# Low halves of second-layer weights: from TensorE to VectorE

## The chip, the cores and the metric

The kernel runs on one core of one Trainium2 chip. The core has five engines that run side by side, each through its own list of instructions in a fixed order, and wait for one another by semaphores: TensorE (PE in the profile), VectorE (DVE), ScalarE (ACT), GpSimd (POOL) and SyncE (SP), which issues all the transfers here. The metric is the device time of one execution in microseconds (us).

## What is computed

A recurrence over 768 positions for 4 x 8 pairs of batch and head (a delta rule with a 48 x 48 state), then two layer pairs on the 3072 tokens:

```python
for t in range(S):
    kt, vt, bt = (k_n[:, :, t], v[:, :, t], beta[:, :, t, None])
    y[:, :, t] = np.einsum('bhd,bhde->bhe', q[:, :, t], state)
    v_old = np.einsum('bhde,bhd->bhe', state, kt)
    state = state + bt[:, :, :, None] * np.einsum('bhd,bhe->bhde', kt, vt - v_old)
...
h = x @ w_in                       # 384 -> 1024
solu = h * softmax(h)
ln = (solu - mu) / np.sqrt(var + 1e-06) * g_ln
x = ln @ w_out                     # 1024 -> 384
...
h = x @ w_in                       # 384 -> 2048, second layer
g = h * (1.0 / (1.0 + np.exp(-1.702 * h)))
out = g @ w_out                    # 2048 -> 384
```

## The kernel before

The sequence is cut into 24 chunks of 32 positions, so that the recurrence becomes 24 steps. Four chunks make a group of 512 tokens. The Plan class gives each piece of work a tag, by which the text names it: `gram` (products of keys with keys and queries, L568, masked by VectorE in L583), `solve` (inverse of a triangular matrix for four chunks on VectorE, with 60 elimination operations in L642 and L645), `rec` (one recurrence step), `A` (first layer and normalisation of one chunk), `B` (first layer's output product of a group, L946) and `C` (second layer of a group, products L981 up and L1008 down).

One recurrence step is a chain over several engines. TensorE forms the state's product with the keys (L748), VectorE subtracts it (L752), in the first four steps TensorE solves twice (L765, then L770 after a copy by ScalarE, and L776 on VectorE), TensorE solves (L757), ScalarE and VectorE copy the result (L782, L786), TensorE forms the output (L792) and the state's update (L827 in the early steps, L822 later), and VectorE adds that to the state (L836), from where the next step goes on. A chunk's layer A then runs through L874 on TensorE, L881 and L893 on VectorE, L890 on ScalarE, and its last lines on GpSimd (L911, L923) and ScalarE. B of a group needs all four chunks; its result is rounded to a high half on ScalarE (L950) and a low half on VectorE (L953), and C needs both. In C, VectorE (L989) and GpSimd (L995) form the halves of the activation.

Products are made of fp16 halves: each operand is high + low, and three of the four products are summed. So each weight tile (128 x 512 of w1 and w2, 128 x 384 of wo1 and wo2; 6 + 8 of the first layer, 12 + 16 of the second) must be turned into two fp16 tiles. The weights arrive as 64-bit floats. Each tile is loaded (L476), rebuilt as fp32 by one ScalarE operation (L479) and three VectorE operations (L481, L483, L491), rounded to the high half by ScalarE (L504), and the low half, the residual, is formed in one of two ways. `PRM["pe"]` is the number of tiles, in the order of their making, that take the first way:

```python
        if nst[0] <= PRM["pe"]:
            bk = Bank((6, 7, 5, 4, 3))

            def rest():
                PE.matmul(bank(bk)[:, 0:n], lhsT=eye[:, (WS, W2S).index(sc)], rhs=fv, start=True, stop=False)
                PE.matmul(bank(bk)[:, 0:n], lhsT=neg, rhs=dh, start=False, stop=True)
            P.add("PE", 1.1 * n / 512, rest, r=fk + [wk + "h", "eye"], w=[bk], prio=prio)
            P.add("ACT", act(n), lambda: ACT.activation(out=dl, in_=bank(bk)[:, 0:n], func=ACTF.Copy),
                  r=[bk], w=[wk + "l"] + over("l"), prio=prio)
        else:
            P.add("DVE", dve(n), lambda: DVE.scalar_tensor_tensor(
                out=dl, in0=fv, scalar=sc, in1=dh, op0=ALU.mult, op1=ALU.subtract),
                r=fk + [wk + "h"], w=[wk + "l"] + over("l"), prio=prio, port=True)
```

The first way is two matmuls, with a scaled unit matrix (L510) and a negative one (L511), and a copy out of PSUM by ScalarE (L513); the second is one VectorE operation (L516).

The order of the work on every engine is set by a planner when the program is built. Each piece has a priority; to it is added an entry of the table `OFF`, by tag and engine. The planner walks through time with its own durations and at each moment starts the ready piece with the lowest priority. Where it expects TensorE to wait before the first C has begun, it puts filler matmuls on zeros into TensorE's list (L351), whose result nobody reads. On the chip each engine only follows its list.

Of the kernel before, what the change touches and what calls it, by code (L numbers as in the profile page):

```python
# [34 lines left out]
PRM = dict(bl=161.965, vm=-0.684, vo=-1.262, pe=38.322, near=22.976, al=0.0, af=0.658, xp=25.764, lp=1.945, go1=24.87, so1=49.904, ew=48, nx=6.743, kp=13.711, need=100.793, fg=0.161, f1=7.669, f3=1796.849, sp=0.084, gp=0.667, gq=99, cold=25.151, cf=-1.14, nb4=9.499, v1b=1.424, cut=0.473, el=22.0, la=0.602, d0=-55.31, d1=-18.518, d2=6.18, d3=1.2, a0=14.438, wo1s=1.606, nk=15.164, nb2=1.269, nb3=7.307, early=21.447, v1=-9.577, wa=0.829, U=36.161, T0=31.882, g0=0.697, a=-0.318, b=0.937, ao=18.661, go=231.282, gs=-2.989, so=-0.04, ss=0.661, w1=-840.745, wo1=-7.28, w2o=-52.255, w2s=8.446, wo2o=41.493, wo2s=4.056, nb=1.319, bs=0.333, cs=4.152, su=8.832, ld=47.69)  # L35
# [24 lines left out]
class Clock:  # L60
# [12 lines left out]
    def behind(self, at):  # L73

        return PRM["need"] * (1.0 - (self.end - at) / self.TICK) - self.sum

# [14 lines left out]
class Plan:  # L91
# [14 lines left out]
    def add(self, eng, dur, fn, r=(), w=(), prio=0.0, lat=0.0, small=False, nb=0.0, work=1.0, port=None):  # L106
        t = Task()
        t.eng, t.dur, t.fn, t.prio, t.lat = eng, dur, fn, prio + OFF.get(self.tag, 0.0) + OFF.get(f"{self.tag}|{eng}", 0.0), lat
        t.deps, t.outs, t.end, t.left, t.ready = set(), [], None, 0, nb
# [26 lines left out]
    def emit(self, sem=SEM, log=None):  # L136
# [6 lines left out]
        top = max(t.work2 for t in self.tasks)  # L143
        if PRM["al"]:
            for t in self.tasks:
                t.prio = (1 - PRM["al"]) * t.prio + PRM["al"] * PRM["af"] * (top - t.work2)
        free = {}
# [19 lines left out]
        while done < n:  # L167
            cand = None
            for e, ts in pend.items():
# [4 lines left out]
                for t in ts:  # L174
                    st = max(e0, t.ready)
                    if t.lat:
                        st = max(st, dma_free - PRM["la"])
                    ok = True
# [22 lines left out]
            if t.eng == "PE":  # L201
                small, near = t.small, t.prio + PRM["near"]
            pend[t.eng].remove(t)
# [5 lines left out]
            if t.eng == "PE":  # L209
                for gate, until, filler in self.fill:  # L210
# [3 lines left out]
                    while True:  # L214
                        clock.run(lo, 0.0, 1.0)
                        if not (st - lo > (PRM["fg"] if clock.warm else 0.5) or clock.warm and clock.behind(lo) > 0.0):
                            break
# [873 lines left out]
```

## Time and profile before

| | us |
|---|---|
| three runs, median | 839.51 |
| lowest and highest of them | 835.08 and 845.69 |
| the profiled execution | 836.79 |
| its span, first to last instruction | 835.1 |
| outside the span | 1.7 |

The profiled execution is one run of its own. Its views give, for each engine, when an instruction ran and what it had waited for. A line number (L516) is that of the kernel's file. Matmuls overlap in TensorE, so that the step from one start to the next tells what one costs there, and not its own duration. In the rows PE is TensorE, DVE VectorE, ACT ScalarE, POOL GpSimd.

### The profile page before, as it was taken

The numbers are of one execution on the slowest core, as the hardware profiler recorded it, in microseconds if no ns is written. First come the engines' busy times: TensorE is split into PE (matmuls) and PEld (weight loads), VectorE is DVE, ScalarE is ACT, GpSimd is POOL, SyncE is SP. The second block draws the span as 40 slices with busy tenths as digits, with TensorE's granted clock in tenths as the row PEclk, the third lists the DMA queues.
The fourth block names the chain that finished last, engine by engine and source line by source line (L and its number), as shares of the span: only waits on it lengthen the run. The fifth ranks groups of instructions, "written<-read, shape, count | busy, mean of one in ns | idle before, by whom it ended". The sixth has DMA issues, their size and how long they took to land.

```text
span 835.1 us, 25208 instructions
## 1 busy us (share of the span) xinstructions
PE 777.1 (93%) x10642; PEld 389.7 (47%) x10642; DVE 589.5 (71%) x1456; ACT 373.1 (45%) x661; POOL 247.2 (30%) x240
## 2 busy tenths in 40 slices
PE   6568978999989999998999999999999999999997
PEld 4135554444555444544544444444444444444443
DVE  2896777999999999999999899964566445212111
ACT  0467564544326524544633545525554355422332
POOL 3020011110413354325531434504442222420322
PEclk7778898999999999999999999999999999999999
DMA  6898597976646466677736654365433252100101
GB/s 168 235 278 232 148 220 137 235 196 168 125 94 139 86 149 171 147 177 159 168 79 187 142 119 104 84 152 144 103 79 94 80 115 44 26 1 0 39 1 38
DMA packets 177314, 105.76 MB, mean 127 GB/s; under 512 B 128273, under 2 KB 161169, under 8 KB 177201
## 3 DMA queue, kind: packets, MB, share of 16 engines
q1 hardware_dynamic: 177200, 104.15, 52.7%
q8 instruction: 83, 1.36, 0.7%
q14 instruction: 31, 0.25, 0.1%
HBM read 66.16 MB, written 20.64 MB: 104 GB/s over the span
## 4 chain that ended last, share of the span: by engine, by line
PE 53%; DVE 27%; issue 9%; DMA 4%; ACT 3%; POOL 2%; POOLq 0%; SPq 0%; ACTq 0%; DVEq 0%
PE psum L1008 13%; PE psum L981 13%; PE psum L946 9%; PE psum L874 6%; DVE mv L836 4%; DVE trip L645 4%; DVE trt L642 4%; PE psum L568 3%; DVE th L989 2%; PE psum L351 2%; DVE mv L786 2%; DVE col L881 2%; PE psum L510 2%; ACT mv L782 2%; DVE eb L893 2%
## 5 line engine op out<-in xcount | busy, mean ns | idle before, releaser
L995 POOL TENSOR_TENSOR gl<-th,gh 128x512 f16<-128x512 f32 x90 | 107.3, 1192 | 236.0 <-ACT gh L992 167.8
L989 DVE SCALAR_TENSOR_TENSOR th<-th,psum 128x512 f32<-128x512 f32 x96 | 65.5, 683 | 89.0 <-ACT th L986 88.4
L1008 PE MATMUL psum<-gl,wo2h 128*128 128x512 f16 x288 | 109.1, 379 | 1.0 <-POOL gl L995 1.0
L1008 PE MATMUL psum<-gh,wo2h 128*128 128x512 f16 x288 | 109.5, 380 | 0.2 <-ACT gh L992 0.2
L981 PE MATMUL psum<-x2th,w2h 128*128 128x512 f16 x288 | 109.5, 380 | 0.1
L981 PE MATMUL psum<-x2th,w2l 128*128 128x512 f16 x288 | 109.1, 379 | 0.0
L981 PE MATMUL psum<-x2tl,w2h 128*128 128x512 f16 x288 | 109.1, 379 | 0.0
L1008 PE MATMUL psum<-gh,wo2l 128*128 128x512 f16 x288 | 109.1, 379 | 0.0
L986 ACT ACTIVATE th<-psum 128x512 f32<-128x512 f32 x96 | 56.9, 593 | 98.4 <-PE psum L981 93.6
L874 PE MATMUL psum<-w1h,xt 128*128 128x512 f16 x288 | 94.2, 382 | 1.5 <-DVE mv L836 0.8
L992 ACT ACTIVATE gh<-th 128x512 f16<-128x512 f32 x96 | 60.2, 627 | 68.9 <-DVE th L989 64.6
L1008 PEld LDWEIGHTS <-wo2h 128*128 128x128 f16 x576 | 56.2, 98 | 67.9 <-issue 2.1
L981 PEld LDWEIGHTS <-w2h 128*128 128x128 f16 x576 | 53.5, 98 | 62.0 <-issue 0.3
L642 DVE TENSOR_TENSOR trt<-trip 128x30 f32<-128x30 f32 (+9 forms) x150 | 71.3, 476 | 2.7
L645 DVE TENSOR_TENSOR trip<-trip,trt 128x30 f32<-128x30 f32 (+9 forms) x150 | 69.6, 464 | 2.4
L923 POOL TENSOR_TENSOR lnr<-eb,lnr 128x1024 f16<-128x1024 f32 x24 | 52.2, 2173 | 52.0 <-ACT lnr L921 52.0
L874 PEld LDWEIGHTS <-xt 128*128 128x128 f16 x432 | 40.0, 98 | 49.9 <-issue 2.5
L890 ACT ACTIVATE eb<-psum,col 128x512 f32<-128x512 f32 x48 | 36.9, 773 | 52.4 <-DVE col L886 52.1
L946 PE MATMUL psum<-lnth,wo1h 128*128 128x512 f16 x144 | 54.6, 379 | 0.4 <-DVE th L989 0.4
L874 PE MATMUL psum<-w1l,xt 128*128 128x512 f16 x144 | 54.8, 381 | 0.0
L946 PE MATMUL psum<-lnth,wo1l 128*128 128x512 f16 x144 | 54.6, 379 | 0.0
L946 PE MATMUL psum<-lntl,wo1h 128*128 128x512 f16 x144 | 54.6, 379 | 0.0
(210 smaller groups left out, 1246.6 us busy)
## 6 DMA issues: line engine op xcount, KB each, us to landing
kq<-kq SPq DMA_DIRECT2D x44, 192.0 KB, 4.4
stg<-w_in SPq DMA_DIRECT2D x11, 512.0 KB, 5.6
vt<-vt SPq DMA_DIRECT2D x24, 192.0 KB, 2.7
st<-qt SPq DMA_DIRECT2D x48, 96.0 KB, 2.9
kt<-kdr SPq DMA_DIRECT2D x48, 96.0 KB, 2.3
stg<-udr SPq DMA_DIRECT2D x48, 96.0 KB, 2.3
out<-ob SPq DMA_DIRECT2D x18, 256.0 KB, 2.7
ktr<-kd SPq DMA_DIRECT2D x46, 96.0 KB, 2.9
```

Of the source, the lines that this page charges most:

```text
L642: DVE.tensor_tensor(out=tv, in0=tri[:, lo:hi, j:j + 1].to_broadcast([128, nr, j]), in1=tri[:, j:j + 1, 0:j].to_broadcast([128, nr, j]), op ...
L645: DVE.tensor_tensor(out=tri[:, lo:hi, 0:j], in0=tri[:, lo:hi, 0:j], in1=tv, op=ALU.add)
L874: PE.matmul(bank(bh[j]), lhsT=x[:, k], rhs=w_[:, k, 512 * j:512 * j + 512], start=(k == 0 and i == 0), stop=(k == K0 - 1 and i == 2))
L890: P.add("ACT", act(512) + 0.34, lambda j=j, ev=ev: ACT.activation(out=ev, in_=bank(bh[j]), func=ACTF.Exp, bias=cl(3), scale=cl(0), accum_o ...
L923: P.add("POOL", pool(F1), lambda: POOL.tensor_tensor(out=lnr[1], in0=e_, in1=lnr[0], op=ALU.subtract), r=["lnrh"] + [f"eb{ie}_{j}" for j i ...
L946: PE.matmul(bank(ba)[:, 0:w_], lhsT=wo1[a][:, k, oc], rhs=lnt[b][:, k, tk], start=(k == 0 and i == 0), stop=(k == K1 - 1 and i == 2))
L981: PE.matmul(bank(bh)[:, 0:w_], lhsT=w2[a][:, k, fc], rhs=x2t[b][:, k, tk], start=(k == 0 and j == 0), stop=(k == K0 - 1 and j == 2))
L986: P.add("ACT", act(w_), lambda: ACT.activation(out=th, in_=bank(bh)[:, 0:w_], func=ACTF.Tanh, scale=0.851 / (X2S * W2S)), r=[bh], w=[f"th{ ...
L989: P.add("DVE", dve(w_), lambda: DVE.scalar_tensor_tensor(out=th, in0=th, scalar=1.0, in1=bank(bh)[:, 0:w_], op0=ALU.add, op1=ALU.mult), r= ...
L992: P.add("ACT", act(w_), lambda: ACT.activation(out=gh, in_=th, func=ACTF.Copy), r=[f"th{i}"], w=[f"gh{i}"], prio=base)
L995: P.add("POOL", pool(w_), lambda: POOL.tensor_tensor(out=gl, in0=th, in1=gh, op=ALU.subtract), r=[f"th{i}", f"gh{i}"], w=[f"gl{i}"], prio= ...
L1008: PE.matmul(bank(acc[o])[:, 0:w_], lhsT=wo2[a][:, f, oc], rhs=gb[i][b][:, 0:w_], start=(f == 0 and j == 0), stop=(f == K2 - 1 and j == 2))
```

## The change

Two tables differ, both one line each in the file; of the first only the start of the old and the new one is shown, of the second all entries but `pe` are equal.

```diff
-OFF = {'gram0|SP': 42.93, 'gram0|PE': 207.21, 'gram0|DVE': 422.4, 'gram1|SP': 9.79,
...
+OFF = {'gram0|SP': -56.29, 'gram0|PE': -67.28, 'gram0|DVE': 69.66, 'gram1|SP': 146.16,
...
-PRM = dict(bl=161.965, vm=-0.684, vo=-1.262, pe=38.322, near=22.976,
...
+PRM = dict(bl=161.965, vm=-0.684, vo=-1.262, pe=14, near=22.976,
...
```

With `pe` at 38.322 the first 38 tiles took the first way: all 14 of the first layer and 24 of the 28 of the second. With 14 only those of the first layer do, and L516 forms the residual of all 28 of the second. The entries of `OFF` are other numbers for nearly every tag and engine, so the order of all the work is another one. In the lists, L351 stands 232 times instead of 128, L510 and L511 belong to 14 tiles instead of 38, L513 stands 14 times instead of 38, L516 28 times instead of 4; all other lines are as many as before. Of the 232 fillers 222 stand ahead of B0, of the 128 126. 

TensorE, from the last state product of the third recurrence step to the fourth step's L770 (L827: state update; L568: a gram; `fst`: a rebuilt weight tile; `eye` and `neg`: the unit matrices). Before:

```order
L827 MATMUL psum_69<-mv,kt_118 48x48 x16
L510 MATMUL psum_68<-fst_88,eye 128x384
L511 LDWEIGHTS neg
L511 MATMUL psum_68<-wo2h,neg 128x384
L568 MATMUL psum_67<-kq_112 32x64 x32
L748 MATMUL psum_70<-mv,ktr_114 32x48 x32
L568 MATMUL psum_69<-kq_111 32x64 x32
L765 MATMUL psum_68<-rb_132,dt_130 32x48 x32
```

The changed kernel, same place, to L770:

```order
L827 MATMUL psum_68<-mv,kt_118 48x48 x16
L568 MATMUL psum_69<-kq_112 32x64 x32
L351 LDWEIGHTS zeros_157
L351 MATMUL psum_63<-zeros_157 128x512
L748 MATMUL psum_68<-mv,ktr_114 32x48 x32
L568 MATMUL psum_69<-kq_111 32x64 x32
L765 MATMUL psum_68<-rb_132,dt_130 32x48 x32
L351 LDWEIGHTS zeros_157
L351 MATMUL psum_63<-zeros_157 128x512
L770 MATMUL psum_69<-vt_121,dt_131 32x48 x32
```

The residual of a tile between L827 and L748 is gone, and a filler on `zeros` stands there and between L765 and L770; the 9 fillers between the first and the fourth step's L765 have become 48, and the 17 residuals in that stretch 2.

VectorE, among the elimination operations of the second solve, around the first L953 (`trip`, `trt`: the triangular matrix; `stg`, `fst`, `ob`: a weight tile as it arrives and as it is rebuilt; `w2l`, `wo2l`: low halves). Before, with the first L516 of all as the last row:

```order
L481 TENSOR_SCALAR stg_84<-stg_84 128x384
L642 TENSOR_TENSOR trt<-trip 128x238
L483 SCALAR_TENSOR_TENSOR fst_89<-fst_89,stg_84 128x384
L645 TENSOR_TENSOR trip<-trip,trt 128x14x17
L491 SCALAR_TENSOR_TENSOR fst_89<-stg_84,fst_89 128x384
L642 TENSOR_TENSOR trt<-trip 128x234
L953 SCALAR_TENSOR_TENSOR x2tl<-psum_66,x2th 128x512
L645 TENSOR_TENSOR trip<-trip,trt 128x13x18
L516 SCALAR_TENSOR_TENSOR wo2l<-fst_89,wo2h 128x384
```

The changed kernel, where the first L953 follows 8 rows further on:

```order
L491 SCALAR_TENSOR_TENSOR fst_87<-wo2l,fst_87 128x384
L642 TENSOR_TENSOR trt<-trip 128x238
L516 SCALAR_TENSOR_TENSOR w2l<-ob_109,w2h 128x512
L645 TENSOR_TENSOR trip<-trip,trt 128x14x17
L516 SCALAR_TENSOR_TENSOR wo2l<-fst_87,wo2h 128x384
L642 TENSOR_TENSOR trt<-trip 128x234
L481 TENSOR_SCALAR stg_84<-stg_84 128x384
```

Here L516 stands among rebuilding and elimination: between the fourth step's L752 and the third L953 there are 13 L516 instead of 1, 60 elimination operations instead of 51 and 38 rebuilding operations instead of 36; ahead of that L752, 9 L516 instead of none and 74 rebuilding operations instead of 87.

## Rows read from the trace of the kernel before

**Rows 1.** The page, part 1: busy us, share of span, instructions.

```profile
PE 777.1 (93%) x10642; PEld 389.7 (47%) x10642; DVE 589.5 (71%) x1456; ACT 373.1 (45%) x661; POOL 247.2 (30%) x240
```

**Rows 2.** Busy time by stretches; columns as the head row says.

```profile
core 0: us, PE busy (x) PEld busy (x) DVE busy (x) ACT busy (x) POOL busy (x), PEclk, DMA share, GB/s
61.60:125.50 63.90, 55.74 (x1504) 35.50 (x1504) 45.23 (x113) 39.98 (x80) 5.75 (x5) 0.88 0.83 203
125.50:175.90 50.40, 45.43 (x837) 24.54 (x834) 42.35 (x122) 23.52 (x40) 8.49 (x6) 0.94 0.94 181
175.90:200.80 24.90, 24.90 (x255) 11.98 (x257) 24.49 (x67) 10.93 (x20) 0.00 (x0) 1.00 0.63 174
200.80:540.00 339.20, 326.55 (x4847) 164.49 (x4836) 317.12 (x778) 155.27 (x271) 133.90 (x120) 1.00 0.60 137
540.00:835.10 295.10, 287.70 (x2629) 135.28 (x2627) 118.95 (x267) 119.06 (x205) 88.12 (x79) 1.00 0.27 65
```

**Rows 3.** Chain that ended last, 55 to 200 us: start, us, what.

```profile
61.62 0.88 PE psum L765 x64
...
125.61 0.95 PE psum L765 x39
...
176.11 11.01 PE psum L946 x51
```

**Rows 4.** Waits of VectorE, 61 to 201 us: total, times, longest.

```profile
DVE rb L776 <- PE psum L770: 10.7, 3, 4.2
DVE rb L752 <- PE psum L748: 4.6, 2, 2.4
```

**Rows 5.** Lines L513 and L516: ns min/median/max, first and last start.

```profile
L513 ACT ACTIVATE wo2l<-psum x12: 468/488/490, 67.3 to 174.6; 128x384 f16<-128x384 f32 x12
L513 ACT ACTIVATE w2l<-psum x12: 582/597/640, 68.3 to 195.1; 128x512 f16<-128x512 f32 x12
...
L516 DVE SCALAR_TENSOR_TENSOR wo2l<-ob,wo2h x2: 549/550/550, 195.6 to 203.1; 128x384 f16<-128x384 f32 x2
```

**Rows 6.** TensorE in order of time: start, us, operation.

```profile
159.00 2.98 PE L351 MATMUL psum<-zeros 128*128 128x512 f16 x13
161.82 1.02 PE L510 MATMUL psum<-fst,eye 128*128 128x512 f32 x2
162.68 0.38 PE L511 MATMUL psum<-w2h,neg 128*128 128x512 f16 x1
162.89 1.67 PE L351 MATMUL psum<-zeros 128*128 128x512 f16 x7
...
172.61 0.81 PE L510 MATMUL psum<-fst,eye 128*128 128x384 f32 x2
173.25 0.33 PE L511 MATMUL psum<-wo2h,neg 128*128 128x384 f16 x1
173.42 0.81 PE L510 MATMUL psum<-ob,eye 128*128 128x384 f32 x2
```

**Rows 7.** VectorE in order of time.

```profile
124.22 0.55 DVE L752 TENSOR_TENSOR rb<-vt,psum 128x384 f32<-128x384 f32 x1 [2.23 <-PE psum L748]
...
132.72 0.56 DVE L776 TENSOR_TENSOR rb<-rb,psum 128x384 f32<-128x384 f32 x1 [4.22 <-PE psum L770]
...
133.86 2.29 DVE L483 SCALAR_TENSOR_TENSOR ob<-ob,stg 128x512 int32<-128x512 int32 x1
...
162.11 0.35 DVE L481 TENSOR_SCALAR stg<-stg 128x384 int32<-128x384 int32 x1
...
163.28 0.56 DVE L483 SCALAR_TENSOR_TENSOR ob<-ob,stg 128x384 int32<-128x384 int32 x1
...
172.49 0.68 DVE L483 SCALAR_TENSOR_TENSOR ob<-ob,stg 128x512 int32<-128x512 int32 x1
...
193.77 0.68 DVE L953 SCALAR_TENSOR_TENSOR x2tl<-psum,x2th 128x512 f16<-128x512 f32 x1
...
200.71 0.68 DVE L989 SCALAR_TENSOR_TENSOR th<-th,psum 128x512 f32<-128x512 f32 x1
```

**Rows 8.** GpSimd in order of time.

```profile
133.43 2.18 POOL L923 TENSOR_TENSOR lnr<-eb,lnr 128x1024 f16<-128x1024 f32 x1 [6.92 <-ACT lnr L921]
```

**Rows 9.** Waits of TensorE, 60 to 130 us.

```profile
PE psum L748 <- issue: 4.8, 2, 2.5
```

More of the change, by code (lines that the diff above doesn't have):

```diff
@@ new lines @@
+PRM = dict(bl=161.965, vm=-0.684, vo=-1.262, pe=14, near=22.976, al=0.0, af=0.658, xp=25.764, lp=1.945, go1=24.87, so1=49.904, ew=48, nx=6.743, kp=13.711, need=100.793, fg=0.161, f1=7.669, f3=1796.849, sp=0.084, gp=0.667, gq=99, cold=25.151, cf=-1.14, nb4=9.499, v1b=1.424, cut=0.473, el=22.0, la=0.602, d0=-55.31, d1=-18.518, d2=6.18, d3=1.2, a0=14.438, wo1s=1.606, nk=15.164, nb2=1.269, nb3=7.307, early=21.447, v1=-9.577, wa=0.829, U=36.161, T0=31.882, g0=0.697, a=-0.318, b=0.937, ao=18.661, go=231.282, gs=-2.989, so=-0.04, ss=0.661, w1=-840.745, wo1=-7.28, w2o=-52.255, w2s=8.446, wo2o=41.493, wo2s=4.056, nb=1.319, bs=0.333, cs=4.152, su=8.832, ld=47.69)
```

3 lines of the change are left out of this document (1 added, 2 removed).

## Prediction

> **What bounds the kernel now.** I read the busy times of the page first. TensorE is busy for 777.1 us, 93% of the span, VectorE for 589.5 us, 71% [rows 1]. That names TensorE, but the share is a mean over stages, so the second view is the table by stretches [rows 2], cut at events that the chain view dates [rows 3]: the first recurrence step starts its matmuls at 61.6, the fourth at 125.6, and B0 (the first layer's output product) starts at 176.1. From 200.8 on TensorE is busy for 326.55 of 339.20 and then 287.70 of 295.10 us: at most 12.7 and 7.4 us of idle time are left to win there, and its real matmuls after B0 are the same in both kernels. So the time is, nearly, the moment at which B0 and C0 can start, plus a fixed queue of matmuls. What can move is the opening.
>
> In the opening TensorE is not short of time though it looks busy. Of its 55.74 us in 61.6 to 125.5 a part is filler matmuls on zeros (L351), and the recurrence is a chain that hops between engines. The waits of VectorE show that: from 61 to 201 it sat 10.7 us in three waits for L770 and 4.6 us in two for L748 [rows 4]; all but the one of 4.22 us before the L776 at 132.72 [rows 7] lie in the first 64 us, where it is idle for 18.7 (63.90 less 45.23) [rows 2]. From 125.5 to 200.8 the picture turns: VectorE is busy for 42.35 of 50.40 and then 24.49 of 24.90 us [rows 2], which leaves 8.5 us. Two stretches, then: the first bound by the hops of the recurrence, the second close to VectorE's limit, with TensorE behind fillers.
>
> **The change, part by part.** *TensorE loses 24 residuals.* In the kernel before 38 tiles get their low half from TensorE and 4 from VectorE; of second-layer tiles, 12 of 512 columns and 12 of 384 go through L513 [rows 5]. From 161.82 to 162.89 is one tile of 512 columns (two passes of L510, one L511), 1.07 us; from 172.61 to 173.42 one of 384, 0.81 us [rows 6]. So 12 x 1.07 + 12 x 0.81 = 22.6 us of TensorE go.
>
> *TensorE gains 104 fillers.* The order of the changed kernel holds 232 fillers, that of before 128. Thirteen of them took from 159.00 to 161.82, 0.217 us each [rows 6]; 104 x 0.217 = 22.6 us. They are fixed instructions, which run whether TensorE has to wait or not. In sum TensorE is handed the same load. By place: between the first and the fourth recurrence step 17 tiles become 2 (about 15.5 us become 1.7) and 9 fillers become 48 (plus 8.5), net 5.3 us less; from the fourth step to B0 8 tiles (7.5 us) go and 57 fillers (12.4 us) come, net 4.9 us more; the rest cancels.
>
> *ScalarE loses 24 evictions,* 12 x 0.597 + 12 x 0.488 = 13.0 us [rows 5]. It is busy for 63.5 of 114.3 us between 61.6 and 175.9 [rows 2], so I count nothing for that; its evictions were short and waited for TensorE.
>
> *VectorE gains 24 operations.* L516 on 384 columns takes 0.55 us [rows 5]. No 512-column L516 ran before; L483 has the same form (two operands in SBUF, 512 columns) and takes 0.68 [rows 7]. That makes 12 x 0.68 + 12 x 0.55 = 14.8 us. Where they stand decides. Counting the order of both kernels up to the fourth step's L752: 87 weight operations before (L481, L483, L491), now 74 plus 9 of L516. At about 0.53 us for a weight operation (0.35 for an L481 of 384 columns, 0.56 and 0.68 for an L483 of 384 and 512) [rows 7] and 0.62 for an L516 (the mean of 0.55 and 0.68), this stretch loses 6.9 and gains 5.6 us, so VectorE does about 1.3 us less. From there to the first L989 stand 11 more L516, one more weight operation and 7 more others: 6.8 + 0.5 + 7 x 0.35 = 9.8 us more (0.35, the time of that L481, is an estimate for the mixed rest, whose operations are mostly smaller than an L483), where 8.5 us of idle time exist.
>
> *What of this is on the path.* First stretch: TensorE's 5.3 us less lie between links of the recurrence: a pair of L510 and L511 between L827 and L748, or between L748 and L765, delays the next link, and 11.1 us of VectorE's waits (10.7 + 4.6 less the 4.22) were for such links. A filler delays less, since it was put where the order expects a wait. I take the 5.3 us as a gain. The bounds are 0 (fillers bite as residuals did) and 13.8 (15.5 less 1.7: fillers only fill waits). Second stretch: the 9.8 us on VectorE either fill its 8.5 us of idle time (a loss of 1.3) or push it all out (9.8); I take the middle, 5.5, because half of its idle time there was the one wait of 4.22 us for L770 [rows 7], which work that stands later in the order cannot fill. The two cancel: 0.2 us.
>
> *After C0 starts,* 6 L516 and 12 weight operations (10.1 us) stand on VectorE up to the sixteenth L989, where before 2 L516 stood (1.4 us); in exchange 6 elimination operations and 19 others stand later. VectorE has 22 us idle from 200.8 to 540 [rows 2] and TensorE almost none, so I take 0; if w2 or wo2 tiles come late for C0 the whole 8.7 us could show as TensorE waiting.
>
> *A price that VectorE pays and TensorE did not.* At 133.86 an L483 took 2.29 us instead of 0.68, while GpSimd ran its L923 from 133.43 to 135.61 [rows 7, 8]. GpSimd is busy for 14.2 of 114.3 us from 61.6 to 175.9 [rows 2], one eighth, so of 24 new operations three would meet it, at up to 1.6 us each: 0 to 5 us, inside the range above. The Trainium skill (SBUF — State Buffer, "SBUF: two separate sides") speaks against the change here: an operation of VectorE with two SBUF inputs and a GpSimd operation that reads SBUF take one port pair in turn, and the later one waits for the whole of the other, whereas TensorE and ScalarE never wait for it. That row agrees with it; by that rule the sum would be 3 us worse than by bare durations.
>
> *The sum.* 836.8 (profiled execution) - 5.3 + 5.5 + 0 = 837.0. The median of the three runs shown is 839.5, 2.7 above the profiled one, so the forecast for the median is **840 us**, no change.
>
> **Rivals.** (a) *The load taken off TensorE is a gain.* If the recurrence was held up by residuals alone, the first stretch gains its whole 13.8 us, VectorE fills its idle time in the second (1.3 lost), and fillers go with a granted clock of 1.00 (all of it at 2.4 GHz), where its mean was 0.88 and 0.94, a mixture with 1.2 GHz [rows 2]; 12 per cent of 56 us and 6 of 45 are another 9 us at most. That gives 839.5 - 13.8 + 1.3 - 6 = 821. Against it: 48 fillers in that stretch say that the order itself expects waits there, and TensorE stopped twice inside running groups of L748 for 4.8 us with no releaser shown [rows 9], which no edit of work removes. (b) *VectorE becomes the bound: slower.* The third L953 (low half of B0's output) is what C0's first matmuls need. In the order it stands behind 13 L516 after the fourth step's L752, before behind one, and behind all 60 elimination operations, before behind 51. If nothing of the first stretch's 5.3 us arrives, the chain from L752 (124.2) to that L953 (193.8) [rows 7] grows by 12 x 0.62 + 9 x 0.35 + 8 x 0.35 + 2 x 0.53 = 14.5 us; TensorE then waits for it with nothing else in its queue, and late tiles add up to 8.7 us. 839.5 + 14.5 + 5 = 859. It decides once B0's start is not earlier than 176 while VectorE has no idle time from 125 on. For it: the 24.49 of 24.90. Against it: 8 us of idle time before, and part of these operations only changes places with later ones. (c) *The change does little because fillers take the residuals' place:* that is the forecast itself.
>
> **How the numbers follow.** A difference under 2% (16.8 us: below 822.7, above 856.3) is about what a measurement of this kernel cannot tell from no change, since its own runs lie from 835.1 to 845.7. Forecast 0.64; (a) 0.18; (b) 0.18. The range has to cover the bounds of the forecast (839.5 - 13.8 + 1.3 = 827, 839.5 + 9.8 + 8.7 = 858) and most of (a): 822 to 859.
>
> **What would show it.** In the profile after: about 232 L351, 14 L513, 28 L516 of 0.55 and 0.68 us; the fourth step's L765 near 120 instead of 125.6; B0 near 173; the first L989 within 5 us of 200.7; VectorE over 95% busy from there back to the fourth step; from 200 on TensorE's idle time still near 20 us. The prediction is wrong if the recurrence speeds up by more than TensorE's 5.3 us, if stops inside groups grow or vanish, or if TensorE's idle time after C0's start grows past 25 us because w2 and wo2 arrive late.

## The result, and the profile after

The changed kernel takes 846.2 us (median of 20 runs, 840.67 to 854.83); the kernel before, run beside it, 839.52 (20 runs, 832.69 to 850.84). The ratio is 1.0085, with a 95% interval from 1.0062 to 1.0108: 5 to 9 us slower, within the 2% that I called no change, inside the range, and 6 us above the forecast of 840. All ratios in this document leave out the runs that are over 1.5% above the fastest of their kernel, so they differ a little from the ratios of the medians. The two profiled spans are 843.9 and 835.1 us, 8.8 apart, a little more than the medians, so a part of what the traces differ by is the luck of two executions.

The page of the changed kernel, busy us of each engine, which answers to [rows 1]:

```profile
PE 780.9 (93%) x10674; PEld 388.7 (46%) x10674; DVE 596.4 (71%) x1480; ACT 363.1 (43%) x637; POOL 251.3 (30%) x240
```

The same stretches as [rows 2], of the changed kernel (the last one to its own end):

```profile
core 0: us, PE busy (x) PEld busy (x) DVE busy (x) ACT busy (x) POOL busy (x), PEclk, DMA share, GB/s
61.60:125.50 63.90, 52.66 (x1615) 31.89 (x1604) 47.35 (x113) 27.89 (x54) 6.18 (x5) 0.91 0.70 173
125.50:175.90 50.40, 47.40 (x727) 25.45 (x726) 41.65 (x133) 21.71 (x35) 9.43 (x6) 0.88 0.93 203
175.90:200.80 24.90, 24.90 (x235) 12.10 (x234) 23.82 (x66) 8.36 (x16) 0.00 (x0) 1.00 0.47 124
200.80:540.00 339.20, 322.25 (x4678) 161.04 (x4678) 314.28 (x753) 154.49 (x271) 131.67 (x117) 1.00 0.61 138
540.00:843.90 303.90, 295.65 (x2814) 139.79 (x2813) 128.26 (x305) 124.46 (x214) 92.19 (x82) 1.00 0.26 65
```

Three things stand in it. TensorE is as busy as before from 61.6 to 200.8 us (125.0 us here, 126.1 before), with 24 residuals less. VectorE, which I had expected over 95% busy from the fourth step on, is busy for 41.65 of 50.40 us from 125.5 to 175.9, less than before, though it has more to do. And from 200.8 to 540 TensorE is idle for 16.95 us, before for 12.65.

The fillers alone (L351) in the first three of these stretches, of the changed kernel; before there were 9, 69 and 2 of them:

```profile
core 0: us, PE busy (x) PEld busy (x), PEclk, DMA share, GB/s
61.60:125.50 63.90, 15.25 (x49) 4.69 (x49) 0.91 0.70 173
125.50:175.90 50.40, 27.83 (x117) 11.21 (x118) 0.88 0.93 203
175.90:200.80 24.90, 3.77 (x17) 1.57 (x16) 1.00 0.47 124
```

VectorE and TensorE in order of time, in the changed kernel: the fourth recurrence step's L752, which stood at 124.22 [rows 7], and its L765, which stood at 125.61 [rows 3]:

```profile
118.96 0.56 DVE L752 TENSOR_TENSOR rb<-vt,psum 128x384 f32<-128x384 f32 x1
119.43 1.98 DVE L491 SCALAR_TENSOR_TENSOR w2h<-wo2l,w2h 128x384 int32<-128x384 int32 x1
...
119.73 0.69 PE L765 MATMUL psum<-rb,dt 32*32 32x48 f32 x42
```

The third L953 and the first L989 on VectorE in the changed kernel [rows 7]:

```profile
196.88 0.69 DVE L953 SCALAR_TENSOR_TENSOR x2tl<-psum,x2th 128x512 f16<-128x512 f32 x1
...
200.69 0.68 DVE L989 SCALAR_TENSOR_TENSOR th<-th,psum 128x512 f32<-128x512 f32 x1
```

The fourth step comes 5.3 us earlier for its L752 (118.96 against 124.22) and 5.9 for its L765; the first L989 comes when it came before (200.69 against 200.71). So in these two traces the 5.3 us are won and spent again between 120 and 200 us. A part of what they are spent on shows in TensorE's stretch ahead of B0 in the changed kernel (the longest run of fillers further ahead as the first row):

```profile
143.01 7.38 PE L351 MATMUL psum<-zeros 128*128 128x512 f16 x30
...
156.32 3.83 PE L351 MATMUL psum<-zeros 128*128 128x512 f16 x17
160.09 1.10 PE L568 MATMUL psum<-kq 48*32 48x64 f32 x64
161.12 2.33 PE L351 MATMUL psum<-zeros 128*128 128x512 f16 x10
163.38 1.10 PE L568 MATMUL psum<-kq 48*32 48x64 f32 x64
164.41 3.84 PE L351 MATMUL psum<-zeros 128*128 128x512 f16 x17
168.18 1.10 PE L568 MATMUL psum<-kq 48*32 48x64 f32 x64
169.21 8.59 PE L351 MATMUL psum<-zeros 128*128 128x512 f16 x39
177.64 0.38 PE L946 MATMUL psum<-lnth,wo1h 128*128 128x512 f16 x1
```

The fillers stand between the Gram products (L568) and end where the first L946 (B0) begins, with no wait named between them. So B0 started when the fillers were through, not when its input arrived: the last two transpositions of that input (L927), issued at 170.19 (`lnth`) and 172.46 (`lntl`), had landed at 174.4 and 175.6.

### The profile page after: what moved, and what is told of

It is laid out like the page before. It is cut to its first block, busy times and chain, and to the rows that moved or that the text cites. A ratio compares the mean times of both kernels' runs of the same rounds, so it can differ in the third digit from the quotient of the medians.

```text
span 843.9 us, 25260 instructions
## 1 busy us (share of the span) xinstructions
PE 780.9 (93%) x10674; PEld 388.7 (46%) x10674; DVE 596.4 (71%) x1480; ACT 363.1 (43%) x637; POOL 251.3 (30%) x240
## 5 line engine op out<-in xcount | busy, mean ns | idle before, releaser
L989 DVE SCALAR_TENSOR_TENSOR th<-th,psum 128x512 f32<-128x512 f32 x96 | 65.2, 682 | 91.4 <-ACT th L986 91.2
L874 PE MATMUL psum<-w1h,xt 128*128 128x512 f16 x288 | 95.0, 388 | 4.3 <-issue 1.6
L642 DVE TENSOR_TENSOR trt<-trip 128x30 f32<-128x30 f32 (+9 forms) x150 | 75.3, 502 | 2.6
L351 PE MATMUL psum<-zeros 128*128 128x512 f16 x232 | 62.0, 416 | 8.0 <-DVE zeros L350 8.0
L874 PEld LDWEIGHTS <-xt 128*128 128x128 f16 x432 | 41.3, 99 | 56.3 <-issue 8.4
L923 POOL TENSOR_TENSOR lnr<-eb,lnr 128x1024 f16<-128x1024 f32 x24 | 52.6, 2194 | 47.3 <-ACT lnr L921 44.1
L874 PE MATMUL psum<-w1l,xt 128*128 128x512 f16 x144 | 55.8, 388 | 0.0
L946 PE MATMUL psum<-lntl,wo1h 128*128 128x512 f16 x144 | 54.6, 379 | 0.9 <-DMA lntl<-lnr 0.9
L836 DVE SCALAR_TENSOR_TENSOR mv<-psum,mv 48x384 f32<-48x384 f32 x92 | 51.1, 555 | 6.2 <-PE psum L822 3.8
```

The source lines that it names most:

```text
L351: P.fill.append((gate, until, lambda: PE.matmul(psum[0], lhsT=z, rhs=z.unsqueeze(1).to_broadcast([128, 4, 128]), start=True, stop=True)))
L642: DVE.tensor_tensor(out=tv, in0=tri[:, lo:hi, j:j + 1].to_broadcast([128, nr, j]), in1=tri[:, j:j + 1, 0:j].to_broadcast([128, nr, j]), op ...
L874: PE.matmul(bank(bh[j]), lhsT=x[:, k], rhs=w_[:, k, 512 * j:512 * j + 512], start=(k == 0 and i == 0), stop=(k == K0 - 1 and i == 2))
L923: P.add("POOL", pool(F1), lambda: POOL.tensor_tensor(out=lnr[1], in0=e_, in1=lnr[0], op=ALU.subtract), r=["lnrh"] + [f"eb{ie}_{j}" for j i ...
L946: PE.matmul(bank(ba)[:, 0:w_], lhsT=wo1[a][:, k, oc], rhs=lnt[b][:, k, tk], start=(k == 0 and i == 0), stop=(k == K1 - 1 and i == 2))
L989: P.add("DVE", dve(w_), lambda: DVE.scalar_tensor_tensor(out=th, in0=th, scalar=1.0, in1=bank(bh)[:, 0:w_], op0=ALU.add, op1=ALU.mult), r= ...
```

## The experiments

All ratios are to the kernel before, run on the same chip beside each; one per cent is 8.4 us, and a range in square brackets is a 95% interval. "In its own order" means that every engine's list is that of the named kernel but for the edit. The first theories were: the loss is VectorE's added load (1), or the other table of offsets (2).

**VectorE's load, down and up, in the changed kernel's own order.**

```
-out=dl, in0=fv, scalar=sc, in1=dh, op0=ALU.mult, op1=ALU.subtract
+(DVE.tensor_scalar(out=dl, in0=dh, scalar1=2.0 ** -11, ...),
+ DVE.scalar_tensor_tensor(out=dl[:, 0:8], in0=fv[:, 0:8], scalar=sc, in1=dh[:, 0:8], ...))
```

> The changed kernel in its own order on every engine, but each of the 28 second-layer L516 is made cheap: an fp16 copy of the high half, scaled by 2^-11, fills the low half, and only its first 8 columns are the residual (so the low halves of the second-layer weights are left out but for these columns). The two small operations should take some 0.3 us in place of 0.55 and 0.68, so VectorE loses about 8 of its 14.8 added us, with TensorE, its fillers and the order untouched. Theory 1 (the added VectorE load, between 60 and 260 us, pushes the later solves back and with them the middle of the kernel): most of the 8.8 us lost behind 300 us comes back, 838 to 841 us, and the third to fifth solves (L663) end earlier than 305, 384 and 467 us. Theory 2 (the loss lies in the other order of the middle, whatever the residuals cost): 845 to 847 us, with the second and third L946 stages where they are in the changed kernel (303 and 434 us).

```
-lambda: DVE.scalar_tensor_tensor(out=dl, ...)
+lambda: [DVE.scalar_tensor_tensor(out=dl, ...) for _ in range(2)]
```

> The changed kernel in its own order, with each of the 28 second-layer L516 issued twice: VectorE gets another 16 to 17 us, nothing else changes. Theory 1 (VectorE load): about as much again as the change lost by this, +7 to +15 us, 853 to 861 us, with the loss again between 60 and 434 us. Theory 2 (order of the middle): within 3 us of the changed kernel, 844 to 849 us.

The light one: 850.15 us, ratio 1.0107 [1.005, 1.0163]; no gain. The small operations took more than I had put down:

```profile
L516 DVE TENSOR_SCALAR wo2l<-wo2h 128x384 f16<-128x384 f16 x16 | 4.0, 251 | 0.0
L516 DVE TENSOR_SCALAR w2l<-w2h 128x512 f16<-128x512 f16 x12 | 3.4, 286 | 3.3 <-ACT w2h L504 3.2
L516 DVE SCALAR_TENSOR_TENSOR w2l<-ob,w2h 128x8 f16<-128x8 f32 x4 | 1.5, 376 | 0.1
L516 DVE SCALAR_TENSOR_TENSOR wo2l<-fst,wo2h 128x8 f16<-128x8 f32 x7 | 1.2, 168 | 0.2
```

These are four groups of VectorE's L516 (busy us, mean ns of one, idle ahead of them); with the rest, L516 takes 13.0 us in all in place of 17.0, so 4 us were taken away, not 8. B1 begins at 304.2, 303.0 in the changed kernel, and the third L946 stage at 435.2 against 434.0. The time meets neither range; the stages lie where theory 2 had them, 1.2 us later. The doubled one: 863.28 us, ratio 1.0276 [1.0224, 1.0328], 1.9% above the changed kernel for 17 us of work, and above the range of theory 1; its B0 comes 6.3 us later (183.9), B1 18.2 later (321.2), and nothing is added behind. So in this order 17 us more on VectorE cost nearly as much, but taking a quarter of the residuals' time away brings nothing that can be measured: theory 1 is not borne out as the main cause, and theory 2 has its stages right but not its time.

**The two parts of the change apart.** The limit alone, and the table alone (PRM's pe 38.322 and 14, OFF of either kernel):

> The change of the residuals alone (limit 14 in place of 38.322) with the table of offsets of the kernel before: 28 L516, 14 L513, 281 fillers, 153 more than before (33 us of them by 0.217 us). Theory 1 (VectorE load): no better than the changed kernel, 846 to 865 us, VectorE the late engine up to 200 us. Theory 2 (the new table costs the time): at or below the time before, 832 to 841 us, since then the old table's middle is kept.

> The new table of offsets alone, with the residuals where they were before (24 more on TensorE, 4 on VectorE; 163 fillers). Theory 1 (VectorE load): VectorE is 14.8 us lighter than in the changed kernel, the opening's gain of 5.3 us stays, so 833 to 841 us. Theory 2 (the new table costs the time): 844 to 852 us, with the loss in the middle (300 to 550 us) as in the changed kernel.

861.06 us, ratio 1.0237 [1.0177, 1.0297], and 865.35 us, ratio 1.0295 [1.0238, 1.0353]. Both are worse than either kernel. The first lies in theory 1's range, the second above both. Each table was made for its own split of the residuals, and a part taken alone is priced with an order that was not made for it. This pair cannot tell where the change's 0.85% come from; kernels with a fixed order can tell more.

**TensorE's residuals and the fillers, each in its own order.**

```
+def rest(w=16 if name in ("w2", "wo2") else n):       # the kernel before
+    PE.matmul(bank(bk)[:, 0:w], lhsT=eye..., rhs=fv[:, 0:w], ...)
+    PE.matmul(bank(bk)[:, 0:w], lhsT=neg, rhs=dh[:, 0:w], ...)
```

> The kernel before in its own order, with its 128 fillers, but the 24 second-layer residual pairs on TensorE (L510, L511) 16 columns wide in place of 512 and 384; ScalarE fills the low half from the high half (scaled by 2^-11) and copies 16 columns from PSUM, so the low halves of these weights are left out but for 16 columns. TensorE loses about 20 of the 22.6 us, and no filler takes their place. Theory A (they lie in stretches that the recurrence or VectorE bounds, as predicted): 836 to 843 us, no verdict. Theory B (in the opening TensorE's time counts one for one): 818 to 825 us. Theory C (they keep the clock up as fillers do): slower, 845 to 852 us, with a granted clock under 0.94 from 125 to 176 us.

```
-                        filler()                       # the changed kernel
+                        self.count += 1; self.count % 9 < 4 or filler()
```

> The changed kernel in its own order, with four of every nine fillers (L351) not issued: 129 in place of 232, about the count before; TensorE has 22.4 us less to do. Theory A (they lie in idle time): 844 to 848 us. Theory B (fillers in the place of residuals take TensorE's time, 4.3 us of it from 176 to 220 us): 838 to 843 us. Theory C (the clock falls without them): 849 to 858 us, with a granted clock below 0.91 and 0.88 in the stretches 61 to 125 and 125 to 176 us.

The narrow residuals: 839.52 us, ratio 0.9969 [0.9931, 1.0006]. Theory A: the 24 residuals cost the kernel before at most 0.7%, where their 22.6 us are 2.7%. The mean granted clock is a little lower, from 0.951 to 0.961 in the runs that the ratio uses and from 0.956 to 0.979 in those of the kernel before beside them. The fewer fillers: 841.34 us, ratio 1.0007 [0.9978, 1.0036]. Against the changed kernel's 1.0085 that is 0.78% less (0.41 to 1.15, the two intervals added as squares), 6.6 us: theory B by its time. The same place on TensorE as above, of this kernel:

```profile
158.60 2.12 PE L351 MATMUL psum<-zeros 128*128 128x512 f16 x9
160.65 1.46 PE L568 MATMUL psum<-kq 48*32 48x64 f32 x64
162.04 5.14 PE L351 MATMUL psum<-zeros 128*128 128x512 f16 x23
171.22 0.59 PE L946 MATMUL psum<-lnth,wo1h 128*128 128x512 f16 x1 [4.04 <-DMA lnth<-lnr]
172.08 0.61 PE L946 MATMUL psum<-lntl,wo1h 128*128 128x512 f16 x1 [0.27 <-DMA lntl<-lnr]
172.48 0.63 PE L946 MATMUL psum<-lnth,wo1l 128*128 128x512 f16 x1
172.90 0.63 PE L946 MATMUL psum<-lnth,wo1h 128*128 128x512 f16 x1
```

B0 now waits for its input, the transpose (L927), and starts at 171.22 instead of 177.64. The input itself comes earlier: its transposition was issued at 165.79, not 170.19. Of these 4.4 us the trace has 3.1 already at the fourth step's L752 (115.87, not 118.96). The first L989 comes at 196.61, 4.1 us earlier; so only 1.0 of them is won between the two. The stretches of this kernel:

```profile
61.60:125.50 63.90, 49.27 (x1613) 31.46 (x1614) 48.41 (x116) 28.86 (x56) 6.63 (x6) 0.90 0.82 192
125.50:175.90 50.40, 40.86 (x691) 21.81 (x690) 45.81 (x138) 21.29 (x35) 9.51 (x6) 0.85 0.97 197
```

From 125.5 to 175.9 TensorE does 6.5 us less and VectorE 4.2 us more (45.81 against 41.65). VectorE had been kept waiting by a TensorE that was multiplying zeros: from 120 to 200 us of the changed kernel it waited 3.5 us for L874, which stood behind 36 fillers (30 of them the run at 143.01), and here 0.5 us. The granted clock falls from 0.88 to 0.85 there, which does not undo the gain.

**Is that so in the kernel before, and is VectorE next?** The same filler edit on the kernel before, and both edits on the changed one:

> The kernel before in its own order, with the same four of every nine fillers not issued: 70 in place of 128, 12.6 us of TensorE work. Theory D (the fillers that the changed kernel has too many of are its own trouble; those of the kernel before lie in idle time): 838 to 843 us beside a before of 841, ratio 0.997 to 1.003. Theory E (fillers in the opening cost in either kernel): 832 to 837 us, the second-layer start (first L946) earlier than 175.9 us. If the clock needs them: 845 to 855 us.

> The changed kernel in its own order with both edits: four of nine fillers not issued, and each second-layer L516 replaced by an fp16 copy scaled by 2^-11 with 8 columns of residual (the low halves of the second-layer weights are left out but for those), some 4.6 us less on VectorE. Theory F (with the fillers out of the way VectorE's load bounds the opening): 836 to 839 us, first L946 near 168 us where fewer fillers alone gave 171.2. Theory G (VectorE's load does not decide at this size): 840 to 843 us, first L946 within 1.5 us of 171.2, and the stretch from the second L946 stage to the third near 132 us in both.

840.07 us, ratio 1.0001 [0.9968, 1.0033], theory D by its time: 12.6 us of fillers fewer, and no gain. They do not all lie in idle time, though: its B0 was 2.8 us earlier (173.1) and its first L989 2.4, but its third L946 stage, with the same instructions behind B0, 1.2 us later than in the trace of before, so the gain was gone there. With both edits 839.57 us, ratio 0.9986 [0.996, 1.0012], B0 at 169.0: 2.2 us earlier than with fewer fillers alone, but 0.2% in the time, inside the intervals. F and G are not told apart.

**VectorE's price by itself, in the kernel before,** and VectorE's work in the middle, in either kernel:

```
+... DVE.scalar_tensor_tensor(out=fi, in0=hi, ..., op1=ALU.bitwise_or) for _ in range(z)]  # z = 2 for the 24 tiles
```

> The kernel before in its own order, residuals on TensorE as they were, but VectorE merges the sign (L491, 0.55 us for 384 columns and 0.68 for 512, the very prices of L516) twice for the 24 second-layer tiles: 14.8 us more on VectorE at the places where the changed kernel adds its residuals, and nothing else. Theory H (VectorE is full from about 120 us to 540 us in either order, so its added work comes through nearly whole): 849 to 856 us beside a before of 841, later solves (L663) by 8 us and more. Theory J (the added VectorE work lies in its idle time, the loss of the changed kernel came from its fillers and its order): 840 to 844 us.

```
-            nr = hi - lo
+            nr, w = hi - lo, min(j, 8) if m > 1 else j     # columns 0:w in place of 0:j
```

> The changed kernel in its own order, with the third to the sixth solve cheaper: their eliminations work on at most 8 columns (the rest of these eliminations is left out), which takes some 15 us of VectorE between 200 and 552 us. Theory H (VectorE bounds the middle, which is why the opening's gain is given back there): 832 to 840 us, less TensorE idle between 220 and 540 us than the changed kernel's 16.2 us. Theory J (order of the middle or fillers alone): 844 to 848 us.

> The kernel before in its own order with the same cheaper eliminations in the third to the sixth solve (the rest of them is left out), some 15 us less VectorE work between 200 and 552 us. Theory H (VectorE bounds the middle of this kernel too): 828 to 836 us. Theory J (TensorE alone sets the end behind 200 us, as the prediction had it): 838 to 843 us.

The 14.8 us on VectorE in the kernel before: 843.35 us, ratio 1.0037 [1.0003, 1.0071], 3.1 us. That is theory J, at its upper end: most of the added work went into the first stretch, as its row shows (56.78 us on VectorE, 45.23 in [rows 2], with 18.7 idle there); the first L989 comes 3.4 us later (204.13):

```profile
61.60:125.50 63.90, 51.42 (x1478) 31.06 (x1476) 56.78 (x134) 40.09 (x81) 5.50 (x5) 0.97 0.85 210
```

The cheaper solves: the changed kernel 843.59 us, ratio 1.0036 [1.0, 1.0072], half a per cent better than 1.0085; its VectorE has 27.6 us less to do behind the first L989, not 15 (415.0 us, in the changed kernel 442.7). The kernel before 837.66, ratio 0.9953 [0.992, 0.9987]. It had 15.0 us less on VectorE (574.5 by its page) and gave back 4.0. So in the middle a microsecond of VectorE is worth about a quarter in the old order and about 0.15 in the new one, both with intervals nearly as wide. Theory H and theory J both miss; the middle is bound by TensorE mostly and by VectorE in part.

The same two kernels show how far two executions differ. Up to the first L989 they run the lists of the changed kernel and of the kernel before unaltered, since the third solve starts behind it. The fourth step's L752 came at 125.84 and 123.33 (118.96 and 124.22 in the first two profiles), the first L989 at 208.10 and 201.26 (200.69 and 200.71).

**A third table.**

> The changed split of the residuals (limit 14) with a third table of offsets, found by a search for this split with the planner's own estimate as its aim (798.9 us by that estimate, which was 802.5 with the changed kernel's table and 799.3 for the kernel before), and four of nine fillers not issued: 140 fillers. If the table of the changed kernel costs what the planner's estimate says, the 3.65 us come off the changed kernel with fewer fillers (ratio 1.0007): ratio 0.994 to 0.998, 836 to 839 us beside a before of 841, faster than both kernels. If the table was no part of the loss, the ratio is again 1.000 to 1.002.

843.97 us, ratio 1.0032 [0.9999, 1.0066]: the gain that the planner's estimate promised did not come. Its estimate orders the two kernels rightly (799.3, 802.5) but is no guide to 0.4%. No kernel that leaves out nothing but fillers was faster than the kernel before.

## Why the prediction was right, and which step was not

The time lies in the range, and no change above 2% was forecast. Of the three terms of the sum (-5.3, +5.5 and 0) the first is not secured, the second was right in size and only in part in its cause, and the third was wrong. That they came so near to the measured time is in part luck.

**The operations: right.** The profile after holds 232 L351, 14 L513, 28 L516. Two of its eight groups of L516, busy us and mean ns:

```profile
L516 DVE SCALAR_TENSOR_TENSOR wo2l<-fst,wo2h 128x384 f16<-128x384 f32 x7 | 3.9, 551 | 0.0
L516 DVE SCALAR_TENSOR_TENSOR w2l<-ob,w2h 128x512 f16<-128x512 f32 x4 | 2.7, 684 | 0.0
```

0.55 and 0.68 us, as L483 had said for 512 columns.

**The first stretch's 5.3 us: met by this trace, not secured.** L752 came 5.3 us earlier, L765 at 119.73 where near 120 was forecast. But another execution of the same opening has L752 at 125.84, later than the 124.22 and 123.33 of the old one: two executions differ by more than the gain. One of my signs of being wrong did come. The stops inside groups of L748 (4.8 us [rows 9]) are gone from 60 to 130 us. TensorE's stops with no releaser shown are now at L792 (3.1), L765 (2.4), L874 (1.6) and L770 (1.5). So another order does remove them, against what I wrote under (a), and as much comes elsewhere.

**The second stretch: its sum right, its cause in part.** From the fourth step's L752 to the first L989, in the kernel before and in the changed one (columns as in [rows 2]):

```profile
124.22:200.71 76.49, 71.52 (x1140) 37.58 (x1132) 68.00 (x191) 34.44 (x60) 8.49 (x6) 0.96 0.85 180
118.96:200.69 81.73, 76.64 (x1152) 40.50 (x1142) 71.83 (x213) 32.21 (x56) 11.47 (x7) 0.92 0.81 173
```

It is 5.2 us longer where I took 5.5, and the second executions agree (77.9 and 82.3). VectorE's term was mis-sized: it is busy for 3.8 us more, not 9.8, and none of that went into its idle time, which is 9.9 us where 8.5 stood before; it is 87% busy from 125.5 to 200.8 where I had forecast over 95%. Its operations overlap, so that durations add up to too much: the L752 at 118.96 takes 0.56 us and the next operation starts 0.47 later; over the whole page 24 operations of 14.8 us raise the busy time by 6.9 (589.5 to 596.4).

The step that failed here is that I put nothing on the 4.9 us that TensorE gains from the fourth step to B0, having written that a filler delays less than a residual, since it was put where the order expects a wait. B0 came at 177.64 instead of near 173, 58.7 us after L752 where it had been 51.7; with four of nine fillers gone it is 55.3. What the rows had to say was there: a run of fillers is as long as the order expected the wait to be, and runs to its end when the wait is shorter. In [rows 6] such runs already stand in the second stretch.

But the fillers are not the whole cause. With four of nine gone as many of them run from L752 to B0 as before (70 and 69), and the stretch to the first L989 is still 80.7 us; with both edits it is 80.3, with the light residuals alone 81.9. Most of its 5.2 us stays with the new order, and which part of the order costs it is not shown.

**After C0's start: 0 taken, and that failed.** Behind the first L989, to the end, in the kernel before, the kernel before with fewer fillers, the changed kernel, and the changed kernel with fewer fillers:

```profile
200.71:835.10 634.39, 614.34 (x7480) 299.86 (x7468) 436.16 (x1045) 274.33 (x475) 222.02 (x198) 1.00 0.44 103
198.27:836.10 637.83, 613.18 (x7422) 298.90 (x7422) 433.40 (x1045) 274.96 (x475) 221.43 (x198) 1.00 0.44 103
200.69:843.90 643.21, 618.01 (x7490) 300.85 (x7488) 442.66 (x1058) 279.06 (x485) 223.86 (x198) 1.00 0.45 104
196.61:839.40 642.79, 615.60 (x7488) 299.62 (x7486) 439.50 (x1058) 278.95 (x485) 223.76 (x198) 1.00 0.46 104
```

All the 8.8 us by which the two profiles differ lie here. With more VectorE work the old order took 640.9; with light residuals the new one took 643.3, and 642.1 with both edits. So the new order takes 1 to 9 us more from there with the same real matmuls, 5.2 in the mean of three traces and four. VectorE is busy there for 6.5 us more (442.66 against 436.16), as I had counted on (8.7); by the 0.15 to 0.25 us that a microsecond of it was worth, that is 1.0 to 1.6 us, an estimate, and not the whole. Fewer fillers bring the first L989 4.1 us earlier than in the kernel before, and that is used up here. Cheaper L516 do not shorten this part; cheaper solves do (638.4), at 27.6 us of VectorE for 4.8. Theory 2, the other order of the middle, is what these traces speak for; what in that order costs the rest stays open.

TensorE's idle time from 200.8 on is 25.2 us (16.95 and 8.25), before 20.0; I had set 25 as the mark of late w2 and wo2 tiles. They are not what TensorE waits for there. Its longest waits from 220 to 545 us in the changed kernel:

```profile
PE psum L792 <- DVE mv L786: 2.6, 9, 0.3
PE psum L1008 <- POOL gl L995: 1.9, 4, 1.3
PE psum L792 <- DVE fst L801: 1.7, 1, 1.7
PE psum L748 <- DVE mv L836: 1.6, 5, 0.3
PE psum L874 <- DMA xt<-ysb: 1.0, 3, 0.5
```

The kernel before with extra VectorE work idled 26.5 us from 200.8 on (18.74 and 7.78), and with fewer fillers 23.9, both in the old order behind B0. So 4 to 6 us of this come and go with how the opening ends, in one order. Of the span's 8.8 us 5.2 are in this idle time; for the other 3.6 TensorE is busy longer with nearly the same matmuls, the largest part in L792 (24.15 us, before 22.42).

**The prices, each with the rest of its kernel's order fixed:** TensorE's 24 residuals gone from the old order, -0.31% (-0.69 to +0.06); 14.8 us more on VectorE in the old order, +0.37% (0.03 to 0.71), 3.1 us, where 17 us more in the new one cost 16; 103 fillers gone from the new order, -0.78% (0.41 to 1.15), 6.6 us, where 58 gone from the old one gave nothing. A price thus holds for its order. That the first two and the 0.78% add up to +0.84%, against the 0.85% measured, shows nothing: the terms come from two orders, and they leave no room for what the new order loses behind the first L989.

**VectorE's stalls against GpSimd: too few to price.** The row of L491 at 119.43 (1.98 us instead of 0.55) is the kind of stall that I meant: GpSimd's L923 ran from 118.76 to 121.00. Of the weight operations on VectorE (L481, L483, L491, L516) two took over 1 us in the changed kernel's trace, none of them an L516, and four in that of before. An L516 can meet it: with doubled residuals one took 2.37 us from 174.60, while L923 ran from 174.33 to 176.55. The 3 us that I had put down by the Trainium skill's rule (SBUF — State Buffer, "SBUF: two separate sides") are not there: nothing here contradicts the rule, but how many operations meet such a stall cannot be had from GpSimd's busy share.

**Rivals.** (a), a gain from the load taken off TensorE: the residuals were worth 0.3%, not 2%. (b), VectorE as the bound: its sign came true, its mechanism in part. From L752 to the third L953 it is 8.4 us longer, not 14.5 (77.9 and 69.5); that L953 came at 196.88, 3.1 us later, and the first L989 no later.

## What to carry to other kernels

Work that one engine is spared is worth what others waited for it, not what the work took: 22.6 us of residuals were worth under 6, in the gaps of a recurrence. Filler work is real work to an engine that runs in order: price each run of it against the wait that it stands for, and look at whether the next real instruction starts with a wait or straight behind the filler. Follow a gain to the end of the kernel before it is counted: 4.1 us won at the first L989 were gone behind it. Run the same list twice before a difference of a few us between two traces is explained. And a table of offsets belongs to the split that it was made for; to price one part of such a change, keep the order and change the instruction, and keep in mind that the price holds for that order.

## What the runs showed that I had not expected

The wait that fillers avoid has a price too. With fewer fillers the changed kernel's TensorE stood still for 4.04 us ahead of B0, and its first matmuls then followed each other by 0.42 us (172.48, 172.90) where 0.216 is usual. The stretches before and after 174.5 us of that kernel, TensorE's busy time and granted clock:

```profile
171.20:174.50 3.30, 3.01 (x7) 0.50 1.02 232
174.50:180.00 5.50, 5.50 (x27) 1.00 0.05 19
```

0.50 is the 1.2 GHz level; seven matmuls in 3.3 us instead of 1.5 are a loss of 1.8 us, 0.27 of it a second wait (for `lntl`). In the changed kernel the run of fillers stands in the same place; the granted clock is 1.00 behind it, but it ended 2 us after the input had landed. And one sequence of instructions, behind different openings, differs more in the middle than the edits do: from the second L946 stage to the third the old order took 125.7 us in the profile of before, 129.9 with fewer fillers and 128.0 with more VectorE work in the opening, while the new order took 130.9 to 132.1 in five kernels.
